# A weight load in longer runs, the copies of the first block shared out, and nine convolution taps moved from VectorE to ScalarE

## The chip, the cores and the metric

One NeuronCore of a Trainium2 chip. The time is device microseconds of a whole execution; the profile's span is some 1.8 us shorter. A few tenths of a microsecond are far below what timed runs of 684 us can tell apart, so most readings rest on places inside the profile. From the first Gelu of block 2 onwards PE never waits long in most of the kernels below, and from there to the first Gelu of block 7 it is 58.33 us in every one of them that has no wait in between (the last experiment, which moves an eviction, apart). So the start of **block 7's first Gelu** tells what a kernel gained or lost, to some 0.01 us.

## The reference

```python
# x (8, 4096, 192), weight (8, 7); 8 heads of 24 channels
w = softmax(weight)                                  # over the 7 taps
y[b, s, c] = sum_k w[head(c), k] * x_pad[b, s + k, c]    # causal, zeros ahead of each sequence
h = y.reshape(32768, 192) @ w_in                     # 192 x 2048
out = gelu_erf(h) @ w_out                            # 2048 x 192, float32 out
```

## The kernel before

The 32768 rows are taken as two halves of 16384, side by side on the two halves of the partitions. Each half is cut into blocks: six of 256 rows (0 to 5), then 29 of 512 (6 to 34). The 192 channels are three *thirds* of 64. For each block VectorE transposes x and does the 7 taps (blocks 0 and 1 do them on PE, as matmuls with diagonal weights, `pconv`), PE multiplies by W_in (`mm1`), ScalarE takes the Gelu, and PE multiplies the block before by W_out (`mm2`) between the slices of `mm1`. A small block has 8 slices, a large one 16. The parts that the change touches:

```python
# which engine copies which piece of block 0's convolution out of PSUM; third 1 comes "exchanged"
# (its two halves on each other's partitions), so it takes two copies of 64 partitions
PIECES = [(0, None), (1, 0), (1, 1), (2, None), (3, 0), (3, 1)]
PA = (0, 3, 4, 5)                     # on ScalarE; 1 and 2 on VectorE

def conv(n, k, p):                    # VectorE: tap k of third p of block n
    ...
    a = acc[:, p * TB : p * TB + w]
    if k == 0:
        ins = v.tensor_scalar(a, src, wk, None, ALU.mult)
    else:
        ...                           # the last tap writes xc, which mm1 reads
        ins = v.scalar_tensor_tensor(dst, src, wk, a, op0=ALU.mult, op1=ALU.add)

# GpSimd's queue: one DMA for all of W_out, 2048 runs of one row (192 bf16, 384 B)
g.dma_start(
    ap(wout, 0, [[NF * C, 128], [C, NF], [1, C]]),
    ap(woutt, 0, [[C, 128], [128 * C, NF], [1, C]]),
).then_inc(S_WOUT, 16)

# TensorE, in block 1: the first matmuls with W_out
if n == 1 and a0 == 0 and a1 > 0:
    t.wait_ge(S_WOUT, 16)

# SyncE: x of blocks 1 and 2 while W_in and W_out still come in, block 3 behind W_out
load(sp, 1)
load(sp, 2)
sp.wait_ge(S_WOUT, 16)
load(sp, 3)
```

## Time and profile before

| | us |
|---|---|
| time, median of 3 (lowest to highest) | 684.04 (683.71 to 684.52) |
| span of the profile | 681.9 |
| 108 to 668 us, PE busy throughout | 559.5 |
| first Gelu of block 0 / 1 / 2 / 7 | 10.62 / 19.39 / 30.39 / 88.73 |

A row of the view by stretch gives busy microseconds of each engine in a window; a row of the timeline gives start, duration, engine, line and operation, with the idle time of the engine and what ended it in brackets. The rows that matter stand in the prediction. VectorE is full for 75 us, and still nobody waits for it.

### The profile page before, as it was taken

What the parts mean: (1) busy time and instruction counts of PE and PEld (TensorE: products, weight loads), DVE (VectorE), ACT (ScalarE), POOL (GpSimd) and SP (SyncE); (2) the same over time, 40 slices, a digit from 0 to 9 for tenths busy, and PEclk for the clock granted to TensorE, in tenths of its full rate; (3) what the DMA queues carried; (4) which work ended last, traced back from release to release, by engine and by line L of the source; (5) the groups of instructions that cost most, each with busy time, mean ns of one, the idle gap of its engine ahead of it and who ended that gap; (6) DMA issues with size and microseconds to landing.
All of it is one profiled execution on the core that took longest, in us unless ns stands there. A gap on an engine that the chain in (4) does not pass through costs nothing.

```text
span 681.9 us, 27319 instructions
## 1 busy us (share of the span) xinstructions
PE 674.9 (99%) x12576; PEld 407.5 (60%) x12576; DVE 564.4 (83%) x918; ACT 535.7 (79%) x548; POOL 20.3 (3%) x51
## 2 busy tenths in 40 slices
PE   8999999999999999999999999999999999999998
PEld 4899655555555555555555555555555555555556
DVE  7999979888889888899888898888898888988611
ACT  7888988777787777787777788777778777778772
POOL 4000000000000000000000000000000000000000
DMA  9345322134432243332234422334421344320123
GB/s 180 76 107 130 83 60 73 43 77 94 96 93 54 47 92 94 95 83 47 62 94 95 94 69 45 79 94 96 94 52 46 95 94 96 77 48 20 48 50 94
DMA packets 133970, 54.00 MB, mean 79 GB/s; under 512 B 128480, under 2 KB 133728, under 8 KB 133856
## 3 DMA queue, kind: packets, MB, share of 16 engines
q1 hardware_dynamic: 129872, 49.93, 31.3%
q0 software_dynamic: 3312, 1.57, 1.8%
q8 instruction: 98, 1.61, 1.0%
q10 hardware_dynamic: 672, 0.76, 0.4%
q14 instruction: 16, 0.13, 0.1%
HBM read 28.66 MB, written 25.17 MB: 79 GB/s over the span
## 4 chain that ended last, share of the span: by engine, by line
PE 96%; ACT 3%; issue 0%; DVE 0%; ACTq 0%
PE hp L743 47%; PE ob L807 43%; PE ob L774 6%; ACT gT L663 2%; PE ob L696 0%; ACT dg L624 0%; ACT osb L257 0%; DVE wcol L474 0%; DVE osb L299 0%; ACT L607 0%; ACT xc L188 0%; ACTq L317 0%; DVE osb L268 0%; ACT wex L611 0%; ACT xTb L632 0%
## 5 line engine op out<-in xcount | busy, mean ns | idle before, releaser
L663 ACT ACTIVATE gT<-hp 128x1024 bf16<-128x1024 f32 x512 | 523.4, 1024 | 131.9 <-PE hp L743 128.6
L743 PE MATMUL hp<-xc,win 64*64 64x512 bf16 (+2 forms) x6048 | 418.4, 366 | 2.0 <-ACT gT L663 1.1
L807 PE MATMUL ob<-gT,wout 64*64 64x512 bf16 x5376 | 366.3, 376 | 0.0
L554 DVE SCALAR_TENSOR_TENSOR acc<-xT,wcol,acc 128x512 f32<-128x512 f32 (+1 forms) x495 | 314.7, 706 | 0.0
L743 PEld LDWEIGHTS hp<-xc,win 64*64 64x64 bf16 (+1 forms) x6048 | 187.8, 106 | 136.2 <-ACT gT L663 2.8
L807 PEld LDWEIGHTS ob<-gT,wout 64*64 64x64 bf16 x5376 | 172.2, 118 | 122.9
L299 DVE STREAM_TRANSPOSE osb<-ob 128x512 f32<-128x512 f32 x84 | 74.2, 886 | 100.8 <-PE ob L807 100.8
L524 DVE STREAM_TRANSPOSE xT<-xin 128x512 f32<-128x512 f32 (+1 forms) x105 | 77.9, 796 | 0.1
L554 DVE SCALAR_TENSOR_TENSOR xc<-xT,wcol,acc 128x512 bf16<-128x512 f32 (+1 forms) x99 | 65.2, 714 | 0.0
L774 PE MATMUL ob<-wout,gT 64*128 64x192 bf16 x1024 | 52.2, 243 | 0.3
L774 PEld LDWEIGHTS ob<-wout,gT 64*128 64x128 bf16 x1024 | 43.6, 94 | 6.3 <-PE ob L774 0.6
L547 DVE TENSOR_SCALAR acc<-xT,wcol 128x512 f32<-128x512 f32 (+1 forms) x99 | 40.6, 467 | 1.2
L434 POOL COPY xT<-xT 128x18 f32<-128x18 f32 x30 | 12.7, 425 | 530.0 <-DVE xT L524 530.0
L270 ACT ACTIVATE osb<-ob 128x192 f32<-128x192 f32 x4 | 1.3, 332 | 9.5 <-PE ob L774 9.5
L268 DVE COPY osb<-ob 128x192 f32<-128x192 f32 x4 | 1.4, 358 | 8.4 <-PE ob L774 8.4
L677 PE MATMUL hp<-warm 128*128 128x512 bf16 x16 | 5.5, 516 | 1.3 <-DVE warm L448 1.3
L257 ACT ACTIVATE osb<-ob 128x384 f32<-128x384 f32 x12 | 5.8, 484 | 0.0
L190 DVE CAST xc<-ob 64x256 bf16<-64x256 f32 (+3 forms) x8 | 3.0, 373 | 1.8 <-PE ob L696 1.7
L677 PEld LDWEIGHTS hp<-warm 128*128 128x128 bf16 x16 | 1.9, 124 | 4.3 <-issue 2.5
L696 PE MATMUL ob<-xTb,dg 64*64 64x256 bf16 (+1 forms) x112 | 3.3, 246 | 0.7 <-ACT xTb L632 0.7
L372 POOL DMA_DIRECT2D win<-in_moe_w_in_dram x6 | 3.9, 654 | 0.0
L696 PEld LDWEIGHTS ob<-xTb,dg 64*64 64x64 bf16 x112 | 2.6, 106 | 1.7 <-ACT xTb L632 1.2
(32 smaller groups left out, 19.2 us busy)
## 6 DMA issues: line engine op xcount, KB each, us to landing
out_dram<-osb SPq DMA_DIRECT2D x122, 192.0 KB, 3.1
xin<-in_x_dram SPq DMA_DIRECT2D x116, 192.0 KB, 4.1
xin<-in_x_dram SPq DMA_DIRECT2D x20, 96.0 KB, 2.5
wout<-in_moe_w_out_dram POOLq DMA_DIRECT2D x1, 768.0 KB, 10.6
win<-in_moe_w_in_dram POOLq DMA_DIRECT2D x4, 96.0 KB, 4.1
win<-in_moe_w_in_dram POOLq DMA_DIRECT2D x2, 192.0 KB, 4.7
out_dram<-osb SPq DMA_DIRECT2D x8, 48.0 KB, 1.7
out_dram<-osb ACTq DMA_DIRECT2D x4, 96.0 KB, 1.9
```

Of the source, the lines that this page charges most:

```text
L257: e.activation(out=dst, in_=src, func=AF.Copy).then_inc(S_EVA)
L299: v.transpose(ap(osb[m % 2], j, [[8 * C, 128], [C // 2, TB // 32], [NP, 32]]), bank(ring(m, j)),).then_inc(S_EV)
L434: g.tensor_copy(dst, src).then_inc(S_HALO)
L524: v.transpose(ap(xT[n % 2], p * XW + HX, [[NP * XW, 128], [1, w]]), ap(xin[n % NX], p, [[TB // 32 * DQ, 128], [D if n == 0 else DQ, w // 3 ...
L547: ins = v.tensor_scalar(a, src, wk, None, ALU.mult)
L554: ins = v.scalar_tensor_tensor(dst, src, wk, a, op0=ALU.mult, op1=ALU.add)
L663: a.activation(out=ap(gT[n % 2], i * c * 2 * w, dst), in_=ap(hp[u % 2], 0, src), func=AF.Gelu,).then_inc(S_GELU)
L677: t.matmul(hp[1][:, 0:512], warm[:, 0:128], warm[:, :])
L696: ins = t.matmul(bank(kd, slice(64 * ho, 64 * ho + 64), w), dg[r, d0 : d0 + 64], xTb[PC[n]][r, x0 : x0 + w], start=(k == KS - 1), stop=(k ...
L743: ins = t.matmul(hp[u % 2][fo : fo + fw, o : o + w], win[r, f1 : f1 + fw], xc[n % 2][r, p * TB : p * TB + w], start=(p == 0), stop=(p == N ...
L774: ins = t.matmul(bank(bb[sub], w=C), gT[m % 2][r, c0 : c0 + 128], wout[r, CH[i] * C : (CH[i] + 1) * C], start=(ph == 0 and i == 0), stop=( ...
L807: ins = t.matmul(bank(ring(m, j), slice(64 * h, 64 * h + 64), w), ap(wout, 64 * hf * NF * C + CH[i] * C + j, [[NF * C, 64], [NP, 64]],), g ...
```

## The change

Three parts. (1) Rows of W_out are interleaved by two, so that one run holds two rows (768 B); as this permutes the rows between the partitions, the columns of W_in are read with a step of two. (2) The two copies of the exchanged third 1 of block 0 go to two engines in place of one, and so do those of the last piece. (3) The first tap of blocks 4 to 6 (a plain multiplication) goes to ScalarE, in slices of two blocks earlier; `acc` is doubled and the transpositions of those blocks are moved half a block ahead, so that ScalarE has its input. The core of the diff:

```diff
+    K0 = {4: 0, 5: 1, 6: 2}
-        acc = sbt("acc", [128, NP * TB], F32)
+        acc = [sbt("acc%d" % i, [128, NP * TB], F32) for i in range(2)]
-        PA = (0, 3, 4, 5)
+        PA = (0, 2, 3, 5)
-                ap(wout, 0, [[NF * C, 128], [C, NF], [1, C]]),
-                ap(woutt, 0, [[C, 128], [128 * C, NF], [1, C]]),
+                ap(wout, 0, [[NF * C, 128], [2 * C, NF // 2], [1, 2 * C]]),
+                ap(woutt, 0, [[2 * C, 128], [256 * C, NF // 2], [1, 2 * C]]),
...
+                ops = [] if n in K0 else [("t", n, p) for p in range(NP)]
+                ops += [("c", n, k, p) for k in range(int(n in K0), KS) for p in range(NP)]
+                if n + 1 in K0:
+                    ops[9:9] = [("t", n + 1, p) for p in range(NP)]
...
+            for n, at in ((4, (3, 5, 6)), (5, (3, 5, 6)), (6, (2, 3, 5))):
+                for p in range(NP):
+                    first[n - 2, at[p]] = (n, p)
+            def first_tap(n, p):
+                a.wait_ge(S_TR, NP * n + p + 1)
+                ...
+                a.activation(out=acc[n % 2][...], in_=ap(xT[n % 2], ...), func=AF.Copy,
+                             scale=wcol[...]).then_inc(S_K0)
...
-                    f0 = 128 * CH[i * c + cc]
+                    f0 = 256 * (CH[i * c + cc] // 2) + CH[i * c + cc] % 2
-                                    win[r, f1 : f1 + fw],
+                                    ap(win, f1, [[NP * F, 64], [2, fw]]),
```

More of the change, by code (lines that the diff above doesn't have):

```diff
@@ L160, in bass_lightweight_conv__then__act_gelu_exact_kernel @@
         S_EVB = sem("S_EVB")
+        S_K0 = sem("S_K0")
         block = es.enter_context(nc.Block())
@@ L194, in wait_pc @@
             if n == 0:
-                e.wait_ge(S_PCA, (1, 1, len(PA))[p])
+                e.wait_ge(S_PCA, (1, 2, 4)[p])
                 if p >= 1:
-                    e.wait_ge(S_PCE, 2)
+                    e.wait_ge(S_PCE, p)
             else:
@@ L206, in cvd @@
         def cvd(n):
-            return NCV * sum(m not in PC for m in range(n + 1))
+            return sum(NCV - NP * (m in K0) for m in range(n + 1) if m not in PC)
         HC = [0]
@@ L534, in conv @@
                 w = WS[n]
-                if k == 0 and p == 0:
+                h = int(n in K0)
+                if k == h and p == 0:
                     v.wait_ge(S_TR, NP * (n + 1))
@@ L538, in conv @@
                     v.wait_ge(S_HALO, HC[n + 1])
-                idx = cvd(n - 1) + NP * k + p
+                idx = cvd(n - 1) + NP * (k - h) + p
                 kt = KS - 1 - k
-                if idx >= NP:
+                if k == h and h:
+                    v.wait_ge(S_K0, NP * K0[n] + p + 1)
+                elif idx >= NP:
                     v.wait_ge(S_CV, idx - NP + 1)
@@ L544, in conv @@
                 wk = wcol[:, p * 32 + kt : p * 32 + kt + 1]
-                a = acc[:, p * TB : p * TB + w]
+                a = acc[n % 2][:, p * TB : p * TB + w]
                 if k == 0:
@@ L557, in conv, with run @@
                 ins.then_inc(S_CV)
-            ops0 = [("t", p) for p in range(NP)] + [
-                ("c", k, p) for k in range(KS) for p in range(NP)
-            ]
-            def run(n, op):
+            plan = []
+            for n in range(2, NB):
+                ops = [] if n in K0 else [("t", n, p) for p in range(NP)]
+                ops += [("c", n, k, p) for k in range(int(n in K0), KS) for p in range(NP)]
+                if n + 1 in K0:
+                    ops[9:9] = [("t", n + 1, p) for p in range(NP)]
+                plan.append(ops)
+            def run(op):
                 if op[0] == "t":
-                    trans(n, op[1])
+                    trans(*op[1:])
                 else:
-                    conv(n, op[1], op[2])
+                    conv(*op[1:])
             diag(0)
@@ L574, in _ @@
             conv_out(v, 0, 1)
-            conv_out(v, 0, 2)
+            conv_out(v, 0, 4)
             dup(1)
@@ L593, in _ @@
             for b in range(2, NB):
-                if b in PC:
-                    continue
-                for o, op in enumerate(ops0):
+                for o, op in enumerate(plan[b - 2]):
                     while side and side[0][0] <= (b, o):
@@ L599, in _ @@
                         side.pop(0)
-                    run(b, op)
+                    run(op)
             for q in side:
@@ L644, in _ @@
                 due[m + 2, 0] = [(m, 1)]
+            first = {}
+            for n, at in ((4, (3, 5, 6)), (5, (3, 5, 6)), (6, (2, 3, 5))):
+                for p in range(NP):
+                    first[n - 2, at[p]] = (n, p)
+            def first_tap(n, p):
+                w = WS[n]
+                a.wait_ge(S_TR, NP * n + p + 1)
+                if p == 0:
+                    a.wait_ge(S_CV, cvd(n - 2))
+                a.activation(
+                    out=acc[n % 2][:, p * TB : p * TB + w],
+                    in_=ap(xT[n % 2], p * XW + HX, [[NP * XW, 128], [1, w]]),
+                    func=AF.Copy,
+                    scale=wcol[:, p * 32 + KS - 1 : p * 32 + KS],
+                ).then_inc(S_K0)
             for n in range(NB):
@@ L649, in _ @@
                     c = NCH[n]
+                    if (n, i) in first:
+                        first_tap(*first[n, i])
                     for k in due.get((n, i), []):
@@ L740, in mm1 @@
                             for fo in range(0, 128, fw):
-                                f1 = p * F + wcols(hf, f0) + fo
+                                f1 = 64 * hf * NP * F + p * F + wcols(hf, f0) + 2 * fo
                                 o = hf * TB + cc * w
```

## The prediction

> **What bounds the kernel now.** I read the page's shares first, then busy time by stretch, then the waits, then the timeline wherever a stretch is not plain PE.
>
> ```profile
> PE 674.9 (99%) x12576; PEld 407.5 (60%) x12576; DVE 564.4 (83%) x918; ACT 535.7 (79%) x548; POOL 20.3 (3%) x51
> ```
>
> ```profile
> 9.00:18.50 9.50, 7.69 (x158) 5.35 (x152) 7.66 (x20) 7.75 (x11) 0.83 (x3) 1.00 1.17 173
> 18.50:29.50 11.00, 10.85 (x224) 9.82 (x226) 10.93 (x30) 8.85 (x10) 0.63 (x2) 1.00 0.36 86
> 29.50:71.50 42.00, 42.00 (x900) 39.73 (x896) 41.89 (x92) 35.02 (x41) 1.07 (x3) 1.00 0.47 108
> 71.50:87.60 16.10, 15.97 (x232) 9.48 (x226) 16.07 (x26) 16.10 (x19) 0.45 (x1) 1.00 0.33 75
> ...
> 108.40:667.90 559.50, 559.50 (x10372) 317.52 (x10364) 461.55 (x702) 442.51 (x433) 10.22 (x25) 1.00 0.32 74
> ```
>
> The columns are the stretch, its length, then busy us of PE, PEld, DVE, ACT and POOL, the granted clock, DMA share and GB/s. From 108 to 668 us PE never rests, at full clock: 192 + 192 matmuls of 512 columns a block, four at a time, one round per 216 ns, 96 rounds = 20.7 us. Nothing in the change removes a matmul, so 560 of the 682 us can't move. What can move lies in the first 88 us: the start-up (9 to 18.5, PE 7.7 of 9.5), the small blocks 1 to 5 (PE full at one slice of 12 + 16 matmuls per 1.315 us), and block 6 (71.5 to 87.6, where ACT is full: 16 Gelus and two evictions).
>
> DVE is also full from 19 to 97 us, and the change is aimed at that. But full is not late. Timeline around the start of block 6 on PE:
>
> ```profile
> 68.46 2.07 DVE L554 SCALAR_TENSOR_TENSOR xc<-xT,wcol,acc 128x512 bf16<-128x512 f32 x3
> ...
> 71.53 0.40 PEld L743 LDWEIGHTS hp<-xc,win 64*128 64x128 bf16 x6
> ```
>
> Block 6's convolution ends at 70.53 and PE's first load for it starts at 71.53, straight after its earlier loads: DVE is 1.0 us early. In the same way it is 1.6 us early for block 7 (86.09 against 87.65), and 3.7 to 6 us for blocks 3 to 5 (block 5: 54.99 against 61.0). The list of waits agrees: what PE waits for is ACT, never the convolution. The longest in sum (us, times, longest):
>
> ```profile
> PEld hp L743 <- ACT gT L663: 2.8, 6, 0.7
> ```
>
> **What the skill says.** (1) "DMA: Bandwidth & Descriptors", Specifications, puts the smallest transfer for line rate at 512 B. W_out goes in runs of 192 bf16 = 384 B; two rows make 768 B. The page agrees that this DMA is slow: 768 KB in 10.6 us is 72 GB/s, though beside x loads also in 384 B runs. (2) "SBUF — State Buffer", Door 1, says reads stay at full rate while at least two accesses fall in a 16-byte line; a step of two bf16 gives four. The trace has a step of three already, on W_out (below). (3) "ScalarE: Activation LUTs", What ACT_TABLE_LOAD costs, gives 0.833 ns per element and some 93 ns for a pointer operand. The trace agrees: a 64-element Copy with a pointer scale takes 332 ns, so 280 fixed. (4) "TensorE: Matmul & The Clock Gate", Step-by-step, says weight loads are pulled ahead of running matmuls. The trace shows it: each load starts with the matmul before its own.
>
> **Part 1, W_out interleaved.** The DMA is issued at 8.15 and releases the sync engine's load of block 3 at 18.75:
>
> ```profile
> wout<-in_moe_w_out_dram POOLq DMA_DIRECT2D x1, 768.0 KB, 10.6
> ```
>
> ```profile
> 18.75 3.81 SPq L317 DMA_DIRECT2D xin<-in_x_dram  x8
> 19.08 0.54 PEld L774 LDWEIGHTS ob<-wout,gT 64*128 64x128 bf16 x12
> ```
>
> PE's first use, at 19.08, follows directly on the loads of the slice before it (18.52 + 0.55): PE did not wait, with 0.3 us to spare. Of block 2's x the last piece lands at 17.24 in the trace's landings, DVE takes it at 17.73. So 1024 fewer packets move both landings earlier, by my estimate 1.5 to 3 us, but both were hidden: 0 us on the path. What they give is room for the start-up to move earlier without meeting a DMA.
>
> The price is that W_in's weights are read with a step of two in all 6048 loads:
>
> ```profile
> L807 PEld LDWEIGHTS ob<-gT,wout 64*64 64x64 bf16 x5376 | 172.2, 118 | 122.9
> L743 PEld LDWEIGHTS hp<-xc,win 64*64 64x64 bf16 x5376 | 157.2, 107 | 127.8 <-ACT gT L663 0.2
> ```
>
> A step of three costs 11 ns a load (118 against 107), and W_out's matmuls keep the same 216 ns rounds as W_in's. A step of two should cost 0 to 11 ns. In the tight stretch (blocks 1 to 5) a load has a slot of 109 ns; after a stall a matmul starts only some 15 ns behind its load, so the true need is far below that slot. 0 us on the path, +0.1 at most.
>
> **Part 2, the copies of block 0.** Now (ACT's copy of third 0 has run from 8.40 to 8.79):
>
> ```profile
> 8.77 0.88 DVE L190 CAST xc<-ob 64x256 bf16<-64x256 f32 x2 [0.19 <-PE ob L696]
> 8.95 0.87 ACT L188 ACTIVATE xc<-ob 128x128 bf16<-128x128 f32 x3 [0.17 <-PE ob L696]
> ...
> 9.72 1.23 PEld L743 LDWEIGHTS hp<-xc,win 64*128 64x128 bf16 x24 [0.76 <-ACT xc L188]
> ```
>
> PE starts at 9.72, once DVE's second piece of third 1 is out (9.65); the last third is out at 9.82. After: DVE has one half of third 1 from 8.77 to 9.20, ACT the other from 8.81 to 9.19. Third 1 is out 0.45 us earlier, PE starts near 9.27. But ACT then still has a 128x128 and a 64x128 piece, at about 0.30 us each (the spacing of the 0.87 for three): 9.80 if they don't overlap, 9.55 if they do. PE waits there in its third pair of matmuls, which ran at 9.96 before: it runs at 9.87, or 9.65. The gain is 0.10 to 0.30 us, taken as 0.15. It lasts: the Gelus of block 0 run back to back from 10.62, later slices wait for them, and block 1's copies and DVE's block 2 follow PE. So all of the rest moves by it.
>
> **Part 3, first taps on ACT.** DVE loses 3 x 0.29 us in blocks 4 and 5 and 3 x 0.40 in block 6 (starts 28.38 to 29.18 and 57.33 to 58.52, plus the spacing): 2.8 us. None was on the path. Also DVE must now wait for the taps: in order, its block 5 would start near 46.2, but the third tap of block 5 sits before Gelu 6 of block 3, near 48.4 + 0.5 = 48.9, two ops after that start: DVE idles some 1.9 us there. Block 6 then ends near 69.6 in place of 70.5: spare time grows by under 1 us, not 2.8.
>
> ACT pays nine taps: by the fixed 280 + 0.833 per element some 0.49 us (256) and 0.71 us (512). Its slots:
>
> ```profile
> 56.30 0.48 ACT L257 ACTIVATE osb<-ob 128x384 f32<-128x384 f32 x1
> 56.69 1.02 ACT L663 ACTIVATE gT<-hp 128x1024 bf16<-128x1024 f32 x1
> 58.01 1.02 ACT L663 ACTIVATE gT<-hp 128x1024 bf16<-128x1024 f32 x1 [0.29 <-PE hp L743]
> ```
>
> A 0.48 us eviction just fits between two Gelus, so a 0.49 us tap fits too. A 0.71 us one puts ACT 0.23 us or more behind. In block 4 that happens at slices 2 and 3, the eviction at 4 recovers nothing, and slice 5 adds a third: 0.69 us behind. PE allows: the Gelu that ends at 59.03 frees a buffer that PE loads for at 59.70; with 0.06 us for the release, 0.61 us. So PE loses 0.1 us there, 0 to 0.3 with the overlap uncertain, and for good.
>
> **Sum.** Part 1: 0. Part 2: -0.15. Part 3: +0.1. That is 684.04 - 0.05 = 684.0. I take 683.8, because the copies may overlap better and the earlier landings remove any wait that falls differently in other executions; this last step is judgement, not a row.
>
> **The rivals.** A, *DVE is the bound and the change frees it*: the 1.0 us of spare time at block 6 would vanish in other executions and 2.8 us of DVE work become up to 1 us of time, 683.0. For it: DVE full from 19 to 97 us. Against: no wait of PE for DVE. B, *ACT becomes the bound*: taps without overlap, or a tap waiting for a late transposition, stall the Gelus: 0.3 to 0.8 us, 684.4 to 684.8. For it: ACT already has only 0.29 us idle per slice. Against: the transpositions are moved ahead and should end 1 to 2 us before their taps. C, *stepped weight loads break the tight stretch*: 10 ns on each of 6 slots in 48 slices is 2.9 us, 687. For it: PEld is at 95% there. Against: the step of three costs no time at the same matmul rate. I give C 4%. D, *the start-up met its DMAs*: W_out's landing, 0.3 us before its use, was the true limit of any gain: then parts 1 and 2 together give 0.3 us, 683.7.
>
> **Range and chances.** A to D without C span 683.0 to 684.8; the three times of before span 0.8 us by themselves. So 683.2 to 684.6. Two per cent is 13.7 us, far from all but a failure of the steady loop: faster 0.01, same 0.98, slower 0.01.
>
> **What would show it.** Right: PE's first load of block 0 near 9.3 and its first Gelu at 10.3 to 10.5; the sync engine's load of block 3 issued at 15.5 to 17; loads of W_in at 107 to 118 ns (64 wide) with rounds of 216 ns; a DVE wait for an ACT tap of about 1.9 us near 47 us; a PE wait for a Gelu under 0.3 us near 60 us; block 6 ready 1 to 2 us early. Wrong: a slice longer than 1.315 us between 30 and 70 us, a Gelu that waits for a tap that waits for DVE, or an end that moves by more than 1 us.

## The result

683.70 us, median of 4 (683.58 to 684.20), against 683.88 us, median of 4 (683.71 to 684.52), of the kernel before: a ratio of 0.9997, 95% interval 0.998 to 1.0014. A ratio here is the mean time of one kernel's fast runs over that of the other's of the same rounds, so it is not quite the ratio of the medians. No difference is resolved. The predicted time was 683.8 us, in a range of 683.2 to 684.6.

That the sum is right doesn't make the steps right. The same stretches as before:

```profile
9.00:18.50 9.50, 8.17 (x158) 5.17 (x152) 6.75 (x18) 7.82 (x11) 0.57 (x3) 1.00 0.99 171
18.50:29.50 11.00, 10.86 (x222) 9.67 (x224) 10.07 (x26) 8.77 (x10) 0.31 (x1) 1.00 0.37 87
29.50:71.50 42.00, 42.00 (x900) 39.74 (x896) 41.42 (x89) 38.11 (x50) 16.59 (x4) 1.00 0.45 108
```

VectorE has lost 0.9 us of busy time in each of the first two stretches, before a single tap of its is saved: it idles. ScalarE has 3.1 us more work from 29.5 to 71.5 (the nine taps), and GpSimd is suddenly busy for 16.6 us in place of 1.1. The waits say what VectorE idled for, and that PE met W_out's landing:

```profile
DVE xT L528 <- DMA xin<-in_x_dram: 2.1, 2, 1.7
...
DVE acc L561 <- ACT acc L667: 0.5, 1, 0.5
...
PEld ob L805 <- DMA wout<-in_moe_w_out_dram: 0.2, 1, 0.2
```

So x of block 2 came 1.7 us too late for VectorE (19.36 us in the landing records; 17.24 before), and W_out at 19.20 (18.73 before), after a change that was to bring both earlier. The start of block 0:

```profile
8.50 1.38 ACT L192 ACTIVATE xc<-ob 128x256 bf16<-128x256 f32 x4 [0.35 <-PE ob L727]
8.79 0.69 DVE L194 CAST xc<-ob 64x256 bf16<-64x256 f32 x2 [0.19 <-PE ob L727]
...
9.34 0.12 PEld L774 LDWEIGHTS hp<-xc,win 64*128 64x128 bf16 x4 [0.36 <-ACT xc L192]
...
10.59 4.93 ACT L694 ACTIVATE gT<-hp 128x1024 bf16<-128x1024 f32 x5 [0.71 <-PE hp L774]
```

PE starts `mm1` at 9.34 (9.72 before), then waits for the last third, and the Gelu starts at 10.59. That is only 0.03 us earlier than before, but the whole start-up ran 0.1 us later in this execution: PE's first convolution weights went in at 7.51 (7.40 before). Counted from there it is 3.08 us in place of 3.21. And the taps, in ScalarE's part of the timeline during block 4:

```profile
53.73 0.71 ACT L667 ACTIVATE acc<-xT,wcol 128x512 f32<-128x512 f32 x1
54.35 1.01 ACT L694 ACTIVATE gT<-hp 128x1024 bf16<-128x1024 f32 x1
...
58.04 0.74 ACT L667 ACTIVATE acc<-xT,wcol 128x512 f32<-128x512 f32 x1
58.65 3.07 ACT L694 ACTIVATE gT<-hp 128x1024 bf16<-128x1024 f32 x3
```

Gelus of this block stood 1.315 us apart before. From the block's first Gelu at 51.50, the sixth would be due at 58.07; it starts at 58.65, 0.58 us late. The next block's first Gelu is on time (62.02 = 51.50 + 8 x 1.315), so PE lost nothing by it. VectorE and PE at block 6:

```profile
68.90 0.74 DVE L561 SCALAR_TENSOR_TENSOR xc<-xT,wcol,acc 128x512 bf16<-128x512 f32 x1
...
71.60 0.40 PEld L774 LDWEIGHTS hp<-xc,win 64*128 64x128 bf16 x6
```

The convolution ends at 69.64, 2.0 us before PE wants it (1.0 before), although VectorE began block 2 1.7 us later.

### The profile page after: what moved, and what is told of

It reads as the page before. It is cut to its first block, busy times and chain, and to the rows that moved or that the text cites. A ratio compares the mean times of both kernels' runs of the same rounds, so it can differ in the third digit from the quotient of the medians.

```text
span 682.0 us, 27319 instructions
## 1 busy us (share of the span) xinstructions
PE 676.2 (99%) x12576; PEld 407.5 (60%) x12576; DVE 562.2 (82%) x909; ACT 538.4 (79%) x557; POOL 35.1 (5%) x51
## 4 chain that ended last, share of the span: by engine, by line
PE 97%; ACT 2%; issue 0%; DVE 0%
PE hp L774 47%; PE ob L838 43%; PE ob L805 6%; ACT gT L694 2%; PE hp L708 1%; PE ob L727 0%; ACT xc L192 0%; ACT osb L261 0%; DVE osb L303 0%; DVE osb L272 0%; DVE warm L452 0%
## 5 line engine op out<-in xcount | busy, mean ns | idle before, releaser
L438 POOL COPY xT<-xT 128x18 f32<-128x18 f32 x30 | 27.9, 930 | 515.3 <-DVE xT L528 492.3
L554 DVE TENSOR_SCALAR acc<-xT,wcol 128x512 f32<-128x512 f32 (+1 forms) x90 | 37.6, 474 | 1.1
L667 ACT ACTIVATE acc<-xT,wcol 128x256 f32<-128x256 f32 (+1 forms) x9 | 5.2, 575 | 0.0
L497 DVE COPY win<-win 64x768 bf16<-64x768 bf16 (+1 forms) x6 | 3.1, 509 | 0.2
```

Source lines behind the costliest of these rows:

```text
L438: g.tensor_copy(dst, src).then_inc(S_HALO)
L667: a.activation(out=acc[n % 2][:, p * TB : p * TB + w], in_=ap(xT[n % 2], p * XW + HX, [[NP * XW, 128], [1, w]]), func=AF.Copy, scale=wcol[ ...
```

## The experiments

The theory after this comparison: part 2 gives its 0.14 us. Part 1 doesn't shorten the loads but shifts them: longer packets give W_out a larger share of the DMA engines, so x of block 2 comes late; part 3 is what makes VectorE bear that. The rivals: the late landing was chance, or came from the new order of rows; VectorE never mattered; the taps cost PE time. Twelve runs followed, two of them repeats. The places of nine profiles, the two of the comparison among them, in us, from the landing records and the timelines (the table is sorted by the length of W_out's packets; "conv" is PE's first convolution weight load, the next three columns are distances, taken from the trace to the nanosecond and then rounded):

| run | W_out packet | conv | to Gelu 0 | to Gelu of block 1 | to Gelu of block 2 | x of block 2 lands | W_out lands | Gelu of block 7 |
|---|---|---|---|---|---|---|---|---|
| before | 384 B | 7.40 | 3.21 | 8.77 | 11.00 | 17.24 | 18.73 | 88.73 |
| before_again | 384 B | 7.43 | 3.20 | 8.78 | 11.11 | 18.01 | 19.26 | 88.86 |
| p23_runs384 | 384 B | 7.42 | 3.08 | 8.97 | 11.23 | 18.26 | 19.44 | 89.04 |
| a384_two_dmas | 384 B | 7.43 | 3.09 | 8.78 | 11.31 | 17.77 | 19.35 | 88.94 |
| p1_interleave | 768 B | 7.44 | 3.26 | 8.87 | 11.00 | 17.99 | 17.77 | 88.89 |
| after | 768 B | 7.51 | 3.08 | 8.79 | 11.08 | 19.36 | 19.20 | 88.79 |
| after_again | 768 B | 7.69 | 3.08 | 8.79 | 11.00 | 18.75 | 18.27 | 88.89 |
| a384_layout | 768 B | 7.46 | 3.08 | 8.79 | 11.00 | 18.79 | 18.62 | 88.66 |
| taps_doubled | 768 B | 7.68 | 3.08 | 8.80 | 11.00 | 18.60 | 18.40 | 90.65 |

**p12_no_taps**: parts 1 and 2 alone.

```diff
-    K0 = {4: 0, 5: 1, 6: 2}
+    K0 = {}
```

> Parts 1 and 2 without the first taps on ScalarE (the table of blocks left empty, all else as in the changed kernel). Theory: with W_out in runs of 768 B the x of block 2 lands near 19.4 us (17.24 before), VectorE starts block 2 1.7 us late, and without the taps it has nothing to give that back with: block 6's convolution ends near 72.2, PE waits some 0.6 us for it near 71.6, and the first Gelu of block 7 starts at 89.3 to 89.5 (88.73 before, 88.79 after the change); time 684.3. Rival: the late landing was chance of one profile; then x of block 2 lands by 17.5, block 6 ends at 70.5, block 7's first Gelu is at 88.6 to 88.8, time 683.7.

684.42 us median; ratio to before 1.0005, 0.9991 to 1.0019. Its profiled execution (710.18 us, clock 0.949) was slow and its places can't be compared, except that there too x of block 2 landed late, at 19.62, 0.24 us after W_out. The four fast times are 684.12, 684.84, 683.67 and 684.42, mean 684.26; the changed kernel's four of the first job have a mean of 683.80, the kernel before in this run's own job one of 683.94. That is the expected direction and size, but within the interval. Inconclusive alone; x2_behind_no_taps below takes it up with x made late on purpose.

**p23_runs384**: parts 2 and 3 alone, W_out and W_in as before (the four changed lines of part 1 put back).

> Parts 2 and 3 without the interleaving: W_out in runs of 384 B and W_in's weights read without a step, as before. Theory: x of block 2 lands near 17.3 and W_out near 18.7, PE does not wait for W_out, and the first Gelu of block 7 starts 0.1 us earlier than after the change, 88.6 to 88.7; VectorE idles about 2.2 us in all for the taps of block 5 (0.54 after the change), and block 6's convolution ends near 69.6, 2 us ahead of PE; time 683.6. Rival (the stepped weights cost time, or the landings have nothing to do with the runs): slices shorter than 1.315 us, or landings at 19.2 to 19.4 again.

683.92 us, ratio 1.0001 (0.9987 to 1.0015). Half right. VectorE waits 1.8 us in all for the taps (expected 2.2, and 1.9 in the prediction), and block 6 is ready at 69.88. x of block 2 landed at 18.26, a microsecond later than expected, but 1.18 us ahead of W_out, where the changed kernel has it behind. The expected 88.6 to 88.7 was missed: W_out landed at 19.44, PE waited for it (11.23 in place of 11.00), and block 1 came 0.2 us late besides (8.97), for which the profile names no cause: it has PE's loads idle for 0.56 us before 18.02, put down to "issue". The slices from block 2 on are as long as in the changed kernel, so the stepped weight loads cost nothing; the loads say the same. In the changed kernel (W_out's first, W_in's second):

```profile
L838 PEld LDWEIGHTS ob<-gT,wout 64*64 64x64 bf16 x5376 | 172.2, 118 | 122.9
L774 PEld LDWEIGHTS hp<-xc,win 64*64 64x64 bf16 x5376 | 157.2, 107 | 127.8 <-ACT gT L694 0.2
```

With a step of two W_in's mean is 107 ns, what it was without a step.

**p1_interleave**: part 1 alone (the four lines on the kernel before).

> The interleaving alone on the kernel before. Theory: x of block 2 lands near 19.4, VectorE's block 2 starts then, block 6 comes 0.6 us late for PE, first Gelu of block 7 at 89.3 to 89.6; W_in's loads of 64 columns stay at 107 ns as they did after the change. Rival (the late landing comes from part 2's earlier copies or from chance): landing by 17.5, first Gelu at 88.7 to 88.8.

683.87 us in one run. My expectation of the landing failed: 17.99, not 19.4, so block 6 was ready at 70.87 and VectorE was not late for it. But W_out landed at 17.77, before x. So "x lands near 19.4" was too narrow a reading of one profile; what holds is the order of the two landings. The 0.09 us that block 1 came late (8.87) is x of block 1: it landed at 12.77 (11.74 before), and VectorE waited 0.73 us for it.

**a384_layout**: the changed kernel with the two rows of a run as a dimension of their own.

```diff
-                ap(wout, 0, [[NF * C, 128], [2 * C, NF // 2], [1, 2 * C]]),
+                ap(wout, 0, [[NF * C, 128], [2 * C, NF // 2], [C, 2], [1, C]]),
```

> The changed kernel with the same interleaved rows, but its one DMA written with the two rows as a dimension of their own, so that it moves runs of 384 B to the same places (2048 packets in place of 1024; a compiler that joins them again would show 768 B packets). Theory (a queue gets its turn by the packet, so long packets take the x load's share): x of block 2 back near 17.3, W_out near 18.7. Rival (the new order of rows, not the length of a run, makes the landing late): 19.2 to 19.4 as after the change. First Gelu of block 7 at 88.6 to 88.8 in both, as the taps cover for VectorE.

683.65 us. The packets are of 768 B: the two rows were joined again, so this run tells nothing of its question and is a repeat of the changed kernel (x 0.17 us after W_out).

**a384_two_dmas**: the same rows in the same places, by two DMAs of every second row.

```diff
+            for r in range(2):
+                g.dma_start(
+                    ap(wout, r * C, [[NF * C, 128], [2 * C, NF // 2], [1, C]]),
+                    ap(woutt, r * C, [[2 * C, 128], [256 * C, NF // 2], [1, C]]),
+                ).then_inc(S_WOUT, 16)        # both waits on S_WOUT: 32
```

> The changed kernel with the interleaved rows loaded by two DMAs, even rows and odd rows, so that the packets really are of 384 B (in the run before, the two rows had been joined again to 768 B). Theory (turns by the packet: with 768 B packets x of block 2 landed 0.16 to 0.23 us after W_out in four profiles, with 384 B packets 1.2 to 1.5 us before it in two): x of block 2 lands 1 to 1.6 us before W_out, the later of the two near 19. Rival (the order of rows matters, not the packets): x of block 2 lands 0.1 to 0.3 us after W_out.

683.93 us. x of block 2 landed at 17.77, 1.58 us before W_out at 19.35. As expected by the theory: with the layout kept and the packets short, the order of landings is that of the kernel before. **before_again** and **after_again** repeat both kernels:

> The kernel before once more, for the spread of the landings from one profile to the next. Theory (384 B packets): x of block 2 lands 1.2 to 1.6 us before W_out, the later near 19, PE's first convolution matmul to block 7's first Gelu 81.3 us or a little more. Rival (17.24 was the rule and the change broke it): x of block 2 at 17.2 again and W_out at 18.7.

> The changed kernel once more, for the same. Theory (768 B packets): x of block 2 lands 0.1 to 0.3 us after W_out, both between 17.8 and 19.6; VectorE waits for it, the taps cover that, and block 7's first Gelu is at 88.6 to 89.0. A landing after 20.0 would hold block 2 itself, as block 2's convolution takes 9.4 us from there and PE wants it at 29.4.

683.81 and 683.89 us. Over the nine profiles of the table, x minus W_out is -1.49, -1.25, -1.18 and -1.58 us with 384 B, and +0.22, +0.17, +0.47, +0.17 and +0.20 with 768 B. One of these, +0.47, lies outside what I had written. The sign never fails. That is what turns by the packet give: x of block 2 is 1024 packets, W_out 2048 of 384 B or 1024 of 768 B. With equal numbers both queues run out nearly together; with half as many, x is through while W_out still has packets left. The Trainium skill, "DMA: Bandwidth & Descriptors", Queues, rings and completion order, says that a DMA engine goes round its queues packet by packet, and that a packet is typically 9 to 17 descriptors. The trace agrees with the turns and shows shorter ones, of one run each. Its packet records name no engine, but a chain of packets at an even distance can be followed. In a384_layout one starts W_out's packets at 17.75, 17.85, 17.94 and 18.03 us and one x packet between each two (17.81, 17.90, 18.00): a turn of 768 + 384 B every 90.5 ns. In a384_two_dmas x and W_out alternate in the same way, 384 + 384 B every 62.4 ns. Per byte that is 12.7 against 12.3 bytes per ns, so the longer packets gave W_out a larger share of each turn and made the whole only some 3% faster.

The mean landing of W_out is 19.20 with 384 B and 18.45 with 768 B; that of x 17.82 and 18.70. So the interleaving brings W_out 0.75 us earlier and x of block 2 0.9 us later. These are means of four and five profiles whose ranges overlap (and 0.6 and 1.0 us if p12_no_taps, left out as slow, is counted). In before_again PE was held by W_out:

```profile
PEld ob L774 <- DMA wout<-in_moe_w_out_dram: 0.2, 1, 0.2
```

Three of the four profiles with 384 B have such a wait (block 1 to block 2 takes 11.11 to 11.31 us), and one of the five with 768 B (11.08). The profile of the kernel before that I predicted from was the exception among its kind.

This decides whether part 2's 0.14 us lasts. The three distances of the table together, from the first convolution load to block 2's first Gelu, are 22.99 and 23.10 us for the kernel before, 23.29 and 23.17 with part 2 and 384 B (p23_runs384, a384_two_dmas), 23.12 with part 1 alone, and 22.87 to 22.95 with both. With short packets PE only waited longer for W_out, in p23_runs384 after a late block 1 besides; with long ones the gain stayed.

**x2_behind** and **x2_behind_no_taps**: x of block 2 made late on purpose, with the taps and without.

```diff
-            load(sp, 2)
             sp.wait_ge(S_WOUT, 16)
+            load(sp, 2)
             load(sp, 3)
```

> The changed kernel, but the sync engine issues the load of block 2's x only after W_out has landed. Theory (in the changed kernel W_out and block 2's x share the DMA engines and both land near 19 us, which is when PE wants W_out; the taps give VectorE room to take x late): W_out lands at 15.3 to 16.8, PE's first use of it follows its earlier loads without a wait; x of block 2 lands at 18.5 to 20 and VectorE starts block 2 then, yet block 6's convolution ends by 70.5, before PE wants it near 71.5; the first Gelu of block 7 comes 81.2 us after PE's first convolution matmul (81.33 before, 81.28 after the change), so near 88.65. Rival (PE was never held by W_out, or VectorE is too late in spite of the taps): no change, or PE waits for the convolution at block 6 and block 7 starts at 89 or later.

> The same late load of block 2's x, without the first taps on ScalarE. Theory (the taps are worth what VectorE was late): from the start of block 2 on VectorE to the end of block 6's convolution it is 52.8 us without taps (17.73 to 70.53 before), so with x at 18.5 to 20 block 6 is ready at 71.3 to 72.8, PE waits 0 to 1.3 us for it, and block 7's first Gelu starts 70.1 us after x of block 2 has landed where that is later than 88.65. With x at 19.5: 89.6, some 1 us behind the run with the taps; time 684.5. Rival (VectorE is never the bound): 88.6 to 88.8 as with the taps.

685.70 us (684.88 to 687.58; ratio 1.0024, 1.001 to 1.0037) with the taps, 687.18 us (686.70 to 687.64; ratio 1.005, 1.0038 to 1.0063) without. W_out landed at 17.05 and 16.96 (15.3 to 16.8 expected) and PE didn't wait for it, as expected. But x landed at 22.19 and 21.61, later than I had estimated, and past another limit: block 2's own convolution takes VectorE 9.37 us (17.73 to 27.10 before), and PE wants it at 29.45, so x has to be there by 20.05 (0.02 to 0.03 us pass from the landing to VectorE's start). Both kernels lost time at block 2, which has no taps on ScalarE. Without taps a second wait follows at block 6:

```profile
74.57 0.36 PEld L776 LDWEIGHTS hp<-xc,win 64*128 64x128 bf16 x6 [1.39 <-ACT gT L696]
74.60 0.82 PE L776 MATMUL hp<-xc,win 64*128 64x512 bf16 x6 [1.19 <-DVE xc L561]
```

The convolution of block 6 ended at 74.45, PE started at 74.57. Block 7's first Gelu came at 91.72; x's landing plus 70.1 is 91.71. With the taps there is no wait at block 6 (its first Gelu 10.51 us after block 5's, against 11.88 without). So the rival, that VectorE is never the bound, is out: without taps the last moment for VectorE's block 2 is 71.53 - 52.8 = 18.73 us, with them it is block 2's own 20.05. The difference of the two kernels' mean times is 1.4 us, or 1.8 without the slowest execution with the taps, the profiled one (687.58 us). That one lost a further 1.3 us between the first Gelus of blocks 2 and 3 (11.81 us in place of 10.52), and the view by stretch shows where:

```profile
28.00:32.00 4.00, 1.84 (x42) 1.57 (x38) 4.00 (x12) 1.76 (x3) 0.00 (x0) 1.00 0.31 74
32.00:36.00 4.00, 4.00 (x56) 3.76 (x52) 3.96 (x12) 1.48 (x2) 0.31 (x1) 0.57 0.52 126
```

PE's weight loads paused for 2.4 us, and the granted clock of the next 4 us was 0.57. In x2_behind_no_taps the pause in the same place was 1.8 us, and the clock stayed at 1.00.

**taps_doubled**: a second copy of each 512-element tap.

```diff
+                if n == 6:
+                    a.activation(out=scr[:, p * TB : p * TB + w], ...)   # same input, same scale
```

> The changed kernel with each of the three 512-element taps of block 6 done twice on ScalarE (the second into a tile that nothing reads). Theory (ScalarE may fall about 0.61 us behind in blocks 1 to 5 before PE has to wait; the three taps used 0.58 of it): three more at 0.62 us each put it 2.4 us behind in sum, PE waits 1.8 us for Gelus of block 4, block 5's first Gelu moves from 62.0 to 63.8, block 7's from 88.8 to 90.6, time 685.5. Rival (the idle 0.29 us of ScalarE before each Gelu is all that it has, so the taps had cost PE already): after the change block 4 had no loss, so this would have to be found as a loss above 1.86 us.

685.63 us. The end of block 4 on ScalarE:

```profile
60.60 2.99 ACT L702 ACTIVATE gT<-hp 128x1024 bf16<-128x1024 f32 x3
63.48 0.49 ACT L262 ACTIVATE osb<-ob 128x384 f32<-128x384 f32 x1
63.88 1.02 ACT L702 ACTIVATE gT<-hp 128x1024 bf16<-128x1024 f32 x1
```

Block 5's first Gelu is at 63.88 (63.8 expected), block 7's at 90.65 (90.6). Nominal would have been 51.60 + 10.52 = 62.12, so PE lost 1.76 us out of 1.86 us of added work. The allowance of about 0.6 us is real: the taps as they are use 0.58 us of it and cost PE nothing, and of the next 1.86 us of ScalarE work 1.76 were paid (so the allowance is 0.58 + 1.86 - 1.76 = 0.68 us).

**wout_halves** and **wout_halves_evict_dve**: a try at a better kernel.

```diff
+            for r in (0, 2, 1, 3):
+                g.dma_start(
+                    ap(wout, 4 * r * C, [[NF * C, 128], [2 * C, 2], [1, 2 * C]]),
+                    ap(woutt, 512 * r * C, [[2 * C, 128], [256 * C, 2], [1, 2 * C]]),
+                ).then_inc((S_WOUT, S_WOUTB)[r % 2], 16)
# second kernel, besides: eviction (5, 0) on VectorE, in the taps of block 7
+            side.append(((NA + 1, 18), evac, v, NA - 1, 0, True))
```

> The changed kernel with W_out brought in four DMAs (in runs of 768 B still) on two semaphores: PE's first matmuls on it wait for the eight blocks of rows that they use first, and for the others only eight units later, near 20.4 us. Theory (W_out's landing near 19 held PE at its first use in most profiles; taken away by an earlier half): the first half lands by 16, the second near 19, PE's first load of W_out's matmuls follows the loads before it, block 2's first Gelu comes 11.0 us after block 1's (11.0 to 11.24 in the profiles so far), and block 7's first Gelu 81.2 us after PE's first convolution matmul, 88.6 to 88.7; time 683.5 to 683.6, at most 0.3 us below the kernel before. Rival (the start-up is held elsewhere): no change to the changed kernel.

> As the run before, and the eviction of block 5 that stands in the middle of block 6 (ScalarE, full there: 16 Gelus and two evictions in 16.1 us) goes to VectorE, in block 7's taps, where the first taps on ScalarE have left it room. Theory (block 6 is bound by ScalarE and the eviction costs it 0.39 us; PE waited 0.36 us for a Gelu at 81.7): that wait goes, block 7's first Gelu starts 0.3 to 0.4 us earlier than in the run before, near 88.3; VectorE's block 7 ends some 0.6 us later, still before PE wants it; time 683.2. Rival (the next eviction or PE itself takes the wait over): 0 to 0.1 us.

684.26 us (ratio 1.0002, 0.9989 to 1.0016) and 683.74 us (0.9997, 0.9984 to 1.001). The first failed: the first half of W_out landed at 17.52 and PE never waited for it, but the last part of W_in now landed at 11.97 (10.15 in the changed kernel) and x of block 1 at 13.95 (12.18), and that held the start-up for more than a microsecond (block 1's Gelu 10.21 us after block 0's, 8.79 in the changed kernel). It is the same exchange once more: what W_out got, the others lost. In the second, x of block 1 landed at 12.98 and 9.17 us were needed; its eviction did what was expected. ScalarE's row runs through the middle of block 6 without one:

```profile
78.70 9.82 ACT L702 ACTIVATE gT<-hp 128x1024 bf16<-128x1024 f32 x10
```

and from block 6's first Gelu to block 7's it is 15.95 us in place of 16.26, 0.31 us less. That is the one gain found here that no load took back, but the time of the kernel as a whole is not told apart from the two others. No version that beats both was shown.

## Why the prediction was right, and where it was not

**The steady loop.** Right: 108 to 668 us is PE alone, 559.5 us before and after.

**Part 2.** Right, in mechanism and size: 0.15 us predicted, 0.14 measured (the mean of 3.21, 3.20 and 3.26 without it is 3.22; 3.08 or 3.09 with it in the table's other profiles). "It lasts" holds in the changed kernel, and not with 384 B packets, where PE then waited for W_out. The absolute place, "first Gelu at 10.3 to 10.5", missed by 0.1 us, because the start-up before it begins anywhere from 7.40 to 7.69 us.

**Part 1, the landings.** Wrong. The step that failed: "1024 fewer packets move both landings earlier, by my estimate 1.5 to 3 us, but both were hidden". W_out comes 0.75 us earlier in the mean, x of block 2 0.9 us later. Fewer packets hardly made the loads shorter (12.7 against 12.3 bytes per ns in the turns; the later of the two landings has a mean of 18.70 us against 19.20, not clear of its spread); they changed whose turn was the larger. "Both were hidden" fell as well: with 384 B packets W_out held PE by 0.1 to 0.3 us in three profiles of four. I took one profile's landings for the kernel's, with 0.3 us of room, where repeats differ by 0.7 us (18.73 to 19.44). Rival D saw that limit and was right in part: part 2's gain was kept only with the longer runs. But both parts together gave 0.1 to 0.2 us to block 2's first Gelu, and not 0.3, and x paid for it.

**Part 1, the stepped loads.** Right: 107 ns, no time. Rival C is out.

**Part 3, VectorE.** "None was on the path" is right for the kernel before and wrong for the changed one. The wait for the taps was predicted at 1.9 us; it is 1.8 us where x is early (p23_runs384) and 0.5 us in the profile after, because the late x had used the rest. Block 6 ready 1 to 2 us early: 2.0. What the prediction missed is that the parts lean on each other: part 1 makes x late, and without part 3 that would have cost what lies past 18.73 us (0.6 us at the 19.36 of the profile after, worked out from the 70.1 us that held in x2_behind_no_taps; p12_no_taps is 0.5 us slower in the mean, not resolved; in the other four profiles with 768 B x came at most 0.06 us past 18.73).

**Part 3, ScalarE.** The mechanism was right and the size off: 0.69 us behind was predicted, 0.58 measured, against an allowance of 0.61. So the +0.1 us is 0. Doubling the taps put the allowance at 0.68.

**The sum.** -0.14 from part 2, 0 from the taps, and -0.3 to +0.1 from W_out's landing, which falls differently each time (PE waits 0 to 0.3 us for it with 384 B, 0 to 0.1 with 768 B). The last step of the prediction, 684.0 to 683.8 "by judgement", named the right reason for the wrong sum: the wait that falls differently in other executions is W_out's. That 683.8 came within 0.1 us of 683.70 is luck, as no difference between the kernels is resolved. Rival A (1 us from a freed VectorE) is out for the kernel before, and holds once x is late. Rival B is out.

**Slips in the working, without effect on the sum.** 768 KB are 786,432 B, so the 10.6 us are 74 GB/s and not 72; the saved taps add up to 2.9 us by the terms given, not 2.8; and after a stall a matmul starts 1 to 5 ns behind its load in most places of the profile (30 ns at 9.72), not 15.

**Left open.** Why block 1 came 0.2 us late in p23_runs384 (the last 16 KB packet of the instruction queue before that gap started at 15.78, the latest of the nine profiles of the table; in before, before_again, p1_interleave and taps_doubled, which have no such gap, it started at 13.5 to 14.6; a late fetch of instructions would fit, but isn't shown); what moves all landings by up to a microsecond from one profile to the next; and how often the changed kernel's x passes 20.05 us, where the taps can't help (19.36 was the latest in five).

## What to carry to other kernels

When several loads are in flight at once, a change of the run length of one is first a change of shares: ask which consumer waits for the one that loses, and look at several profiles before you call a landing hidden. An engine that is full but early has a last moment, and it can be worked out from one profile (when its consumer wants the result, less the length of its work); compare that with when its input can come. An engine with two buffers between it and the bottleneck has a fixed allowance of delay: work placed inside it is free, the next piece is paid almost in full.

## What the Trainium skill lacked or had wrong

- "DMA: Bandwidth & Descriptors", Specifications, gives 512 B as the least for line rate. Between 384 and 768 B the turns above show almost no step: 12.3 bytes per ns with W_out in 384 B, 12.7 in 768 B, each beside an x packet of 384 B. And 384 B is not one rate: a chain of W_out packets alone starts one every 32 ns (before, before_again), some 12 bytes per ns, a chain of x packets alone one every 19 ns (after, from 18.56 us), some 20. What makes the two queues differ isn't shown.
- The same page, Queues, rings and completion order, has packets of typically 9 to 17 descriptors between turns; here the queues of W_out and x changed after every run (90.5 ns for one of 768 B and one of 384 B in a384_layout).
- "SBUF — State Buffer", Who interferes with whom, describes the lock that VectorE and GpSimd share as held for one instruction. After the change, with the transposition no longer between, a GpSimd copy of 18 elements was caught in a row of VectorE instructions with two inputs and lasted until the next transposition at 69.57, eighteen instructions later; the next one, beside other work, took its usual time:

```profile
57.77 11.93 POOL L438 COPY xT<-xT 128x18 f32<-128x18 f32 x1 [9.25 <-DVE xc L561]
72.09 0.45 POOL L438 COPY xT<-xT 128x18 f32<-128x18 f32 x1 [2.39 <-DVE xT L528]
```

  It cost nothing here, as its result was wanted at 73.19 only. An earlier one, among nine such instructions, lasted 3.56 us (39.37 to 42.93, the next transposition at 42.79). p12_no_taps and p1_interleave, which keep the transposition where it was, have no copy above 0.45 us in these blocks.
- "TensorE: Matmul & The Clock Gate", What's actually happening, says that the clock drops after an idle window of some 3.4 us. In x2_behind a pause of 2.4 us in PE's weight loads was followed by a mean granted clock of 0.57 over 4 us; a pause of 1.8 us in x2_behind_no_taps was not (1.00).
